# Linear attention, a top-2 mixture of experts and a feed-forward layer in one kernel: decoding spread over two steps, square sums in pieces, earlier input tiles, spread checks

## The chip, the cores and the metric

The kernel runs on one core of one Trainium2 chip. The metric is the device time of one execution in microseconds (us). TensorE (PE) multiplies matrices, VectorE (DVE) and ScalarE (ACT) work element by element, GpSimd (POOL) issues the gathering transfers and SyncE (SP) nearly all others. Each engine works through its own queue in order.

## What is computed

Three layers on 3072 tokens (4 batches of 768) of width 384: a gated linear attention with 8 heads, a mixture of 8 experts of which each token takes two, and a feed-forward layer with h - tanh(h) in place of an activation.

```python
def _attn_ref(q, k, v, f_logit):
    f = 1.0 / (1.0 + np.exp(-f_logit))
    for t in range(S):
        state = f[:, :, t, :, None] * state + np.einsum('bhd,bhe->bhde', k[:, :, t], v[:, :, t])
        y[:, :, t] = np.einsum('bhd,bhde->bhe', q[:, :, t], state)

def _moe_ref(x, w_gate, w_noise, noise, w1, w2):
    noisy_logits = x @ w_gate + np.log1p(np.exp(x @ w_noise)) * noise
    top2 = np.argpartition(-noisy_logits, 2, axis=1)[:, :2]
    ...
            h = np.maximum(x[mask] @ w1[e], 0.0)
            out[mask] += top2_w[mask, k, None] * (h @ w2[e])

def _moe2_ref(x, w_in, w_out):
    h = x @ w_in
    g = h - np.tanh(h)
    return (g @ w_out).astype(np.float32)
```

## The kernel before

The order of the work is written out by hand: each engine's queue has the instructions in the order in which the Python code issues them. Three stages follow each other.

The **attention** (lines 250 to 546) works in 24 chunks of 128 tokens and routes them on the way; the routed rows are scattered to `xs` in memory, expert by expert.

The **experts** are 128 steps (line 662): expert e, block `blk` of its 832 slots, slice f of 128 of the 1024 hidden columns. The blocks have 512 and 320 slots; in the last expert (e = 7) 320 and then 512. `moe_first` (204) makes the first product of a step, `ph`, out of nine matmuls, since every number is held as two 16-bit halves; ScalarE then writes the upper half of `hs`, VectorE the lower. `moe_second` (222) makes the second product two steps later (`LAG`), into the sums `py`; after the last slice ScalarE and VectorE move `py` to `yo`, which goes to `y_rows` in memory. Beside the products a step carries other work: `load_weights` (132) and `split_weights` (141) bring the next expert's weights into 16 buffers of two halves; `weight_sums` (148) squares them and adds up, for a check; every second step `decode_work` (582) turns 64-bit numbers of the last layer's weights into 32-bit ones: a square on ScalarE, four operations on VectorE, then for `w_in` scaling on ScalarE (591) and the lower half on VectorE, and, for the last chunk of each of three rows of tiles, a square over 2048 columns (594). For `w_out` the result goes to memory, `wo_f32`, and comes back as the weights of "expert" 8. In the last block of the last expert `gather_y` (599) fetches for each tile of 128 tokens the two experts' rows, `combine` (606) adds them with their weights, and `put_m` (612) splits the sum, has it transposed into the input tile of the feed-forward and squares it for a check.

The **second feed-forward** (line 751) has 6 blocks of 512 tokens with 16 slices each, 96 steps. In a step TensorE makes the first product of step n (`ff_first`, 621) and the second product of step n - 3 (`ff_second`, 642, `FF_LAG`). ScalarE squares `ph` to `z` and `z` to `s`, VectorE makes `s` and `g`, ScalarE the upper and VectorE the lower half of `hs` (`ff_split`, 635). The next block's four tiles are gathered at step 0 of a block, combined at 4, 6, 8 and 10 and put at 7, 9, 11 and 13. Three blocks' input tiles `xt` are held. Steps 0 to 7 also square the weights of expert 8 (764).

The fast way is only right for inputs in certain ranges; the sums are compared with bounds (`check_routes` at step 20, the rest at the end, 772 to 780), the verdicts multiplied into `ok`, added up over the partitions by a matmul, and the result is the `flag` (783). Every engine loads it and branches; where a check fails, a slow general way follows. The lines at the foot of the loop:

```python
        if n < M:
            ff_split(blk, f)
            if n < 8:
                weight_sums(NE, n)
            if n == 20:
                check_routes()
        if n < M and blk < 5 and f in (4, 6, 8, 10):
            combine(4 * blk + 4 + (f - 4) // 2)
        if n < M and blk < 5 and f in (7, 9, 11, 13):
            put_m(4 * blk + 4 + (f - 7) // 2)
```

Of the kernel before, what the change touches and what calls it, by code (L numbers as in the profile page):

```python
# [55 lines left out]
XSUM = 1.0e9  # L56
# [15 lines left out]
def fast(ctx, tc, flag, f_cols, kq_cols, v_rows, gates, blank, w12, w_in, w_out, out):  # L72
# [43 lines left out]
    isum = consts.tile([128, 3], F32, name="isum")  # L116
    xsum = consts.tile([128, 2 * NE], F32, name="xsum")
    hacc = consts.tile([128, 16 * NE], F32, name="hacc")
    msum = consts.tile([128, NT], F32, name="msum")
    junk = consts.tile([128, F2], F16, name="junk")  # L120
# [27 lines left out]
    def weight_sums(e, f):  # L148
        for i in range(2):
            nc.scalar.activation(junk[:, :DM], RING[e, f][:, 0, 3 * i:3 * i + 3, :].rearrange("p a b -> p (a b)"),  # L150
                                 AF.Square, accum_out=wsum[:, 8 * e + f, i:i + 1])
# [52 lines left out]
    def moe_first(e, blk, f):  # L204
# [376 lines left out]

    def decode_work(kind, i):
        n = 192 if kind else 256
        o = dec.tile([128, 256], F32, name="wdec")[:, :n]
        decode(o, (kind, i), n)
        if kind:
            nc.sync.dma_start(rows(wo_f32, i // 2 * 128 * DM + i % 2 * 192, [[DM, 128], [1, 192]]), o)
        else:
# [4 lines left out]
            if c == 7:  # L593
                nc.scalar.activation(junk, winS[:, 0, a, :], AF.Square, accum_out=isum[:, a:a + 1])
# [17 lines left out]
    def put_m(j):  # L612
# [6 lines left out]
        nc.scalar.activation(junk[:, :DM], g1, AF.Square, accum_out=msum[:, j:j + 1])  # L619
# [42 lines left out]
    for n in range(3, len(moe_steps) + LAG):  # L662
# [42 lines left out]
        if 4 < n < 8:  # L705
            decode_load(*loads_ahead.pop(0))
    dctx.close()
# [10 lines left out]
    def check_routes():  # L718
# [3 lines left out]
        holds(1, dv, 0.0, OP.is_lt)  # L722
        holds(4, lgs[:, :, 8:16], NMAX, OP.is_le)
# [6 lines left out]
        nc.vector.tensor_scalar(total[:, 0:1], total[:, 0:1], float(2 * N), None, op0=OP.is_equal)  # L730
# [4 lines left out]
        holds(5, sums, WSUM[0], OP.is_ge)  # L735
        holds(6, sums, WSUM[1], OP.is_le)
# [14 lines left out]
    for n in range(M + FF_LAG):  # L751
# [8 lines left out]
        if n >= FF_LAG:  # L760
            ff_second(*steps[n - FF_LAG])
# [305 lines left out]
```

## Time and profile before

| | |
|---|---|
| median of 3 runs | 996.01 us (993.24 to 997.07) |
| the profiled execution | 992.07 us, its span 990.2 us |
| granted clock of TensorE, mean | 0.985 |
| busy: PE, DVE, ACT, POOL | 948.7, 616.5, 606.6, 154.6 us |
| attention; experts; feed-forward; closing | to about 158; to 581; to 977; to 990 us |

The span is the time from the first to the last instruction of the profiled execution. A busy time is the sum over an engine's instructions; matmuls are pipelined, so two that follow each other overlap a little. The number in brackets behind a row of a timeline is the idle time ahead of it, and behind the arrow stands what ended it.

### The profile page before, as it was taken

Reading aid. Unit: us, or ns where it says so; the run is one execution under the profiler, and the core shown is the slowest. Engines: PE = TensorE matmul, PEld = TensorE weight load, DVE = VectorE, ACT = ScalarE, POOL = GpSimd, SP = SyncE. Lnnn points to the kernel's source line nnn. Section 1 sums busy time; section 2 is a strip of 40 time slices with the busy share of each in tenths; the row PEclk is TensorE's granted clock in tenths of the full one; section 3 lists DMA queues with packets and bytes.
Section 4 is the critical chain, followed back from the end, with each engine's and each line's share of the span. In section 5 each row is a group of like instructions: output and inputs, shape, how many; then the busy total and the mean of one; then the engine's idle time right before and its main releaser. Section 6 shows DMA issues by size and latency. Waiting matters only on the chain.

```text
span 990.2 us, 16233 instructions
## 1 busy us (share of the span) xinstructions
PE 948.7 (96%) x5970; PEld 580.2 (59%) x5970; DVE 616.5 (62%) x1267; ACT 606.6 (61%) x1511; POOL 154.6 (16%) x194
## 2 busy tenths in 40 slices
PE   8999999999999999999998899889899999999994
PEld 8999986555556565656565454445445555555552
DVE  7899995465555556666766434567656566666553
ACT  5777763665647475757576776654656656566552
POOL 2377776000000000000000321200201101000000
PEclk8999999999999999999999999999989999999998
DMA  7877755764636464754544341210211202100001
GB/s 256 279 239 255 257 164 169 201 188 118 193 117 194 125 180 156 178 174 143 157 140 131 77 115 53 72 56 1 73 56 37 60 33 56 41 17 17 32 1 36
DMA packets 111801, 120.04 MB, mean 121 GB/s; under 512 B 66400, under 2 KB 89568, under 8 KB 111584
## 3 DMA queue, kind: packets, MB, share of 16 engines
q1 hardware_dynamic: 105568, 100.03, 34.2%
q0 software_dynamic: 6144, 18.88, 6.0%
q8 instruction: 49, 0.80, 0.3%
q14 instruction: 40, 0.33, 0.1%
HBM read 76.41 MB, written 29.88 MB: 107 GB/s over the span
## 4 chain that ended last, share of the span: by engine, by line
PE 77%; ACT 10%; DVE 9%; DMA 2%; issue 2%; POOL 0%; SPq 0%; DVEq 0%; ACTq 0%
PE py L201 32%; PE ph L186 31%; PE pY L366 4%; PE pA L339 2%; PE pt L410 2%; PE pY L364 2%; PE pK L383 2%; ACT s L629 2%; DVE s L630 2%; DVE g L632 2%; ACT junk L150 2%; ACT hs L638 2%; ACT z L628 1%; PE pkr L352 1%; ACT hs L211 1%
## 5 line engine op out<-in xcount | busy, mean ns | idle before, releaser
L201 PE MATMUL py<-wsplit,hs 128*128 128x384 f16 x2432 | 435.2, 327 | 11.3 <-ACT yo L236 3.9
L201 PEld LDWEIGHTS <-hs 128*128 128x128 f16 x2432 | 236.9, 98 | 189.3 <-ACT hs L638 6.4
L186 PE MATMUL ph<-xt,wsplit 128*128 128x512 f16 (+3 forms) x1152 | 223.5, 339 | 0.5 <-DMA xt<-xs 0.5
L186 PE MATMUL ph<-xt,winS 128*128 128x512 f16 x864 | 205.2, 384 | 10.3 <-DMA xt<-m 9.5
L186 PEld LDWEIGHTS <-wsplit 128*128 128x128 f16 x1152 | 112.6, 98 | 86.7 <-DMA xt<-xs 0.8
L218 DVE SCALAR_TENSOR_TENSOR hs<-ph,hs 128x256 f16<-128x256 f32 (+2 forms) x192 | 79.7, 443 | 123.8 <-ACT hs L211 123.1
L638 ACT ACTIVATE hs<-g 128x512 f16<-128x512 f32 x96 | 60.4, 629 | 145.9 <-DVE g L632 145.9
L186 PEld LDWEIGHTS <-winS 128*128 128x128 f16 x864 | 84.9, 99 | 105.3 <-issue 14.4
L602 POOL DMA_INDIRECT g<-y_rows,yslot x48 | 46.5, 969 | 610.2 <-ACT junk L150 385.3
L211 ACT ACTIVATE hs<-ph 128x512 f16<-128x512 f32 (+3 forms) x128 | 65.5, 512 | 107.9 <-PE ph L186 107.4
L630 DVE SCALAR_TENSOR_TENSOR s<-s,z 128x512 f32<-128x512 f32 x96 | 66.5, 692 | 91.0 <-ACT s L629 91.0
L639 DVE TENSOR_TENSOR hs<-g,hs 128x512 f16<-128x512 f32 x96 | 66.4, 692 | 63.3 <-ACT hs L638 63.3
L145 DVE SCALAR_TENSOR_TENSOR wsplit<-raw,wsplit 128x768 f16<-128x768 f32 x72 | 70.3, 977 | 18.0 <-ACT wsplit L144 16.7
L150 ACT ACTIVATE junk<-wsplit 128x384 f16<-128x384 f16 x144 | 74.6, 518 | 2.6
L629 ACT ACTIVATE s<-z,bias_a 128x512 f32<-128x512 f32 x96 | 69.3, 722 | 3.1
L632 DVE SCALAR_TENSOR_TENSOR g<-s,ph 128x512 f32<-128x512 f32 x96 | 65.9, 687 | 3.3
L628 ACT ACTIVATE z<-ph 128x512 f32<-128x512 f32 x96 | 56.1, 584 | 12.6 <-PE ph L186 12.3
L144 ACT ACTIVATE wsplit<-raw 128x768 f16<-128x768 f32 x72 | 60.0, 833 | 1.0 <-DMA raw<-in_w 0.9
L479 POOL DMA_INDIRECT xs<-xkeep,yslot x48 | 55.2, 1151 | 15.5 <-issue 8.7
L366 PE MATMUL pY<-v,am 128*128 128x48 f32 x384 | 54.5, 271 | 0.0
L366 PEld LDWEIGHTS pY<-v,am 128*128 128x128 f32 x384 | 50.8, 196 | 0.1
L325 POOL TENSOR_TENSOR kqT<-eneg,kq 128x512 f32<-128x512 f32 x23 | 32.6, 1420 | 17.2 <-ACT eneg L321 16.9
(137 smaller groups left out, 891.9 us busy)
## 6 DMA issues: line engine op xcount, KB each, us to landing
raw<-in_w SPq DMA_DIRECT2D x64, 384.0 KB, 3.9
kq<-in_kq_cols SPq DMA_DIRECT2D x24, 512.0 KB, 5.5
y_rows<-yo SPq DMA_DIRECT2D x47, 192.0 KB, 2.3
f<-in_f_cols SPq DMA_DIRECT2D x24, 256.0 KB, 3.9
w<-in_moe_w_out SPq DMA_DIRECT2D x32, 192.0 KB, 3.5
w<-in_moe_w_in SPq DMA_DIRECT2D x24, 256.0 KB, 3.5
v<-in_v_rows SPq DMA_DIRECT2D x24, 192.0 KB, 2.6
out<-o SPq DMA_DIRECT2D x24, 192.0 KB, 1.9
```

The source lines that it names most:

```text
L145: nc.vector.scalar_tensor_tensor(t[:, 1], raw, SW, t[:, 0], op0=OP.mult, op1=OP.subtract)
L150: nc.scalar.activation(junk[:, :DM], RING[e, f][:, 0, 3 * i:3 * i + 3, :].rearrange("p a b -> p (a b)"), AF.Square, accum_out=wsum[:, 8 * ...
L186: nc.tensor.matmul(ph[:, :n], l, x[:, r, :n], start=(o == 0), stop=(o == 8))
L201: nc.tensor.matmul(p[:max(m, 128)], l, r, start=(f == 0 and o == 0), stop=(f == last and o == len(ops) - 1))
L211: nc.scalar.activation(hs[:, :n], ph[:, :n], AF.Relu, accum_out=hacc[:, at:at + 1])
L218: nc.vector.scalar_tensor_tensor(hs[:, at:at + hi - lo], ph[:, lo:hi], 0.0, hs[:, lo:hi], op0=OP.max, op1=OP.subtract)
L366: nc.tensor.matmul(pY[:, at + 48 * s:at + 48 * s + 48], am[:, s, a, :], vt[:, 2 * a + s, :], start=not c, stop=bool(s) or not c)
L629: nc.scalar.activation(s, z, AF.Square, scale=1.0 / SZ, bias=bias_a)
L630: nc.vector.scalar_tensor_tensor(s, s, ZD, z, op0=OP.add, op1=OP.mult)
L632: nc.vector.scalar_tensor_tensor(g, s, 0.5, ph, op0=OP.mult, op1=OP.mult)
L638: nc.scalar.activation(hs[:, :512], g, AF.Copy)
L639: nc.vector.tensor_tensor(hs[:, 512:], g, hs[:, :512], op=OP.subtract)
```

## The change

The arithmetic of the result stays; what moves is when and in what pieces the side work is done.

- **Decoding over two steps.** `decode_work` ends with the decoded tile and notes it in `DEC`; `decode_put`, at the next even step, stores or scales it. The squares of `w_in` are taken over 512 columns after every second chunk instead of 2048 after the last (`isum` gets four columns for each row of tiles).
- **Square sums in pieces.** The input's squares (`xsum`) come in three pieces at f = 2, 4, 6 instead of one at 7. `weight_sums` becomes `weight_sum` for one half. The 32 halves of experts 7 and 8 move into the feed-forward, one a step: at steps 13, 14, 15 and 0 of blocks and in the last block. The square in `put_m` becomes `sum_m`, at steps 9 to 12 (those of block 0's own tiles in steps 0 and 1).
- **Weights of expert 8** are split in the second half of expert 7, not the first.
- **Input tiles sooner.** `combine` at steps 1, 3, 5, 7 and `put_m` at 2, 4, 6, 8 of a block.
- **Checks** are a generator that gives one check a step in the last block; `last_check` takes the last six columns of `hsum`.
- **Flag.** The product that makes the flag stands ahead of the last second product on TensorE.

```diff
-XSUM = 1.0e9
+XSUM = 3.0e8
...
-        if f == 7:
-            nc.scalar.activation(junk[:, :3 * n].rearrange("p (a t) -> p a t", a=3), XT[e, blk][:, :3, :n], AF.Square,
-                                 accum_out=xsum[:, 2 * e + blk:2 * e + blk + 1])
+        if f in (2, 4, 6):
+            a = f // 2 - 1
+            nc.scalar.activation(junk[:, :n], XT[e, blk][:, a, :n], AF.Square,
+                                 accum_out=xsum[:, 2 * e + blk, a:a + 1])
...
+    DEC = []
+
     def decode_work(kind, i):
         n = 192 if kind else 256
         o = dec.tile([128, 256], F32, name="wdec")[:, :n]
         decode(o, (kind, i), n)
+        DEC.append((kind, i, o))
+
+    def decode_put(kind, i, o):
         if kind:
...
-            if c == 7:
-                nc.scalar.activation(junk, winS[:, 0, a, :], AF.Square, accum_out=isum[:, a:a + 1])
+            if c % 2:
+                nc.scalar.activation(junk, winS[:, 0, a, (c - 1) * 256:(c + 1) * 256], AF.Square,
+                                     accum_out=isum[:, a, c // 2:c // 2 + 1])
...
-        if blk == 1 if e == 0 else blk == 0:
+        if blk == (e in (0, NE - 1)):
             if f < 6:
                 load_weights(e + 1, f + 2)
             split_weights(e + 1, f)
-        if blk == 1:
-            weight_sums(e, f)
-            if f >= 6 and e + 2 <= NE:
+        if f >= 6:
+            if e < NE - 2 and blk == 1:
                 load_weights(e + 2, f - 6)
+            if e == NE - 1 and blk == 0:
+                load_weights(NE, f - 6)
+        if blk == 1 and e < NE - 1:
+            weight_sum(e, f, 0)
+            weight_sum(e, f, 1)
+        if DEC and not f % 2:
+            decode_put(*DEC.pop(0))
...
+        if n == M + FF_LAG - 1:
+            p = ps.tile([1, 1], F32, name="pt", tag="b7")
+            nc.tensor.matmul(p, ok, ones[:, 0:1], start=True, stop=True)
+            nc.vector.tensor_scalar(flag, p, 128.0, None, op0=OP.is_lt)
         if n >= FF_LAG:
             ff_second(*steps[n - FF_LAG])
...
+        if n >= M:
+            continue
+        ff_split(blk, f)
+        if blk < 5:
+            if f in (1, 3, 5, 7):
+                combine(ahead + f // 2)
+            if f in (2, 4, 6, 8):
+                put_m(ahead + f // 2 - 1)
+            if f in (9, 10, 11, 12):
+                sum_m(ahead + f - 9)
+        else:
+            next(checking, None)
+        if halves and (blk == 5 or f == 0 or f > 12):
+            weight_sum(*halves.pop(0))
+        if n < 2:
+            sum_m(2 * n)
+            sum_m(2 * n + 1)
+        if n == M - 1:
+            ok = last_check()
```

How instructions move, at three places. ScalarE in the first half of the last expert, two steps before the change (`hs` is the upper half, `wsplit` a weight split, `wsq` and `winS` the decoding):

```order
L211 ACTIVATE hs,hacc<-ph 128x320
L144 ACTIVATE wsplit<-raw 128x768
L211 ACTIVATE hs,hacc<-ph 128x320
L144 ACTIVATE wsplit<-raw 128x768
L575 ACTIVATE wsq<-w_6141 128x256
L591 ACTIVATE winS<-wdec 128x256
L594 ACTIVATE junk,isum<-winS 128x2048
```

and after it:

```order
L210 ACTIVATE hs,hacc<-ph 128x320
L575 ACTIVATE wsq<-w_6178 128x256
L210 ACTIVATE hs,hacc<-ph 128x320
L213 ACTIVATE junk,xsum<-xt 128x320
L596 ACTIVATE winS<-wdec 128x256
L599 ACTIVATE junk,isum<-winS 128x512
```

The scaling `winS` is no longer right behind the square `wsq` of the same chunk, but behind the next step's `hs`, and the splits are gone from here. ScalarE in the first two steps of the feed-forward before the change:

```order
L628 ACTIVATE z,hsum<-ph 128x512
L629 ACTIVATE s<-z,bias_a 128x512
L638 ACTIVATE hs<-g 128x512
L150 ACTIVATE junk,wsum<-wsplit 128x384 x2
L628 ACTIVATE z,hsum<-ph 128x512
```

and in its first four steps after it:

```order
L637 ACTIVATE z,hsum<-ph 128x512
L638 ACTIVATE s<-z,bias_a 128x512
L647 ACTIVATE hs<-g 128x512
L149 ACTIVATE junk,wsum<-wsplit 128x384
L628 ACTIVATE junk,msum<-g_6587 128x384
L628 ACTIVATE junk,msum<-g_6591 128x384
L637 ACTIVATE z,hsum<-ph 128x512
L638 ACTIVATE s<-z,bias_a 128x512
L647 ACTIVATE hs<-g 128x512
L614 ACTIVATE g_6824<-g_6824,wt 128x384
L628 ACTIVATE junk,msum<-g_6595 128x384
L628 ACTIVATE junk,msum<-g_6599 128x384
```

Two weight squares behind each of eight steps give way to one square, a combine or a put behind nearly every step; only the first two carry more. VectorE at the very end before the change (`held` and `okay` are the checks):

```order
L639 TENSOR_TENSOR hs<-g,hs 128x512
L654 TENSOR_SCALAR o<-py_9811 128x384
L654 TENSOR_SCALAR o<-py_9819 128x384
L715 TENSOR_SCALAR held<-msum 128x24
L716 TENSOR_REDUCE okay<-held 128x1
```

and after it:

```order
L648 TENSOR_TENSOR hs<-g,hs 128x512
L732 TENSOR_SCALAR held<-hsum 128x6
L733 TENSOR_REDUCE okay<-held 128x1
L737 TENSOR_TENSOR okay<-okay 128x1
L732 TENSOR_SCALAR held<-hsum 128x6
L733 TENSOR_REDUCE okay<-held 128x1
L794 TENSOR_TENSOR ok<-okay 128x1
L816 TENSOR_SCALAR flag<-pt 1x1
L663 TENSOR_SCALAR o<-py_9807 128x384
L663 TENSOR_SCALAR o<-py_9815 128x384
```

The checks stood behind the moves of the last output tiles; now the last two and the flag stand ahead of them.

## Rows read from the trace of the kernel before

**Rows 1.** The page: the span, and TensorE's part of it.

```profile
span 990.2 us, 16233 instructions
...
PE 948.7 (96%) x5970; PEld 580.2 (59%) x5970; DVE 616.5 (62%) x1267; ACT 606.6 (61%) x1511; POOL 154.6 (16%) x194
```

**Rows 2.** Waits of TensorE (PE): in total, times, longest, in us.

```profile
PE ph L186 <- DMA xt<-m: 9.5, 2, 4.7
```

**Rows 3.** Chain that ended last, 450 to 730 us: start us, us, what.

```profile
451.55 1.22 PE ph L186 x9
452.77 1.30 PE py L201 x8
...
466.68 1.94 PE ph L186 x9
...
475.11 1.95 PE py L201 x12
...
533.29 2.00 ACT junk L594 x2
```

**Rows 4.** Timeline of PE, 480 to 660 us; idle time and its releaser in brackets.

```profile
532.97 1.39 PE L186 MATMUL ph<-xt,wsplit 128*128 128x320 f16 x9
535.76 1.61 PE L201 MATMUL py<-wsplit,hs 128*128 128x384 f16 x8 [1.40 <-ACT hs L211]
...
554.03 3.68 PE L201 MATMUL py<-wsplit,hs 128*128 128x384 f16 x12 [3.88 <-ACT yo L236]
...
581.10 7.93 PE L186 MATMUL ph<-xt,winS 128*128 128x512 f16 x36
```

**Rows 5.** Timeline of ScalarE (ACT), 488 to 600 us: decoding, then the first steps.

```profile
540.45 0.42 ACT L591 ACTIVATE winS<-wdec 128x256 f16<-128x256 f32 x1 [2.54 <-DVE wdec L580]
...
583.24 0.60 ACT L628 ACTIVATE z<-ph 128x512 f32<-128x512 f32 x1 [2.12 <-PE ph L186]
...
587.33 0.52 ACT L150 ACTIVATE junk<-wsplit 128x384 f16<-128x384 f16 x1
...
587.85 0.58 ACT L628 ACTIVATE z<-ph 128x512 f32<-128x512 f32 x1
```

**Rows 6.** Timeline of PE, 640 to 730 us: the second and third block begin.

```profile
649.34 3.79 PE L186 MATMUL ph<-xt,winS 128*128 128x512 f16 x9 [4.73 <-DMA xt<-m]
...
719.56 4.00 PE L186 MATMUL ph<-xt,winS 128*128 128x512 f16 x9 [4.73 <-DMA xt<-m]
```

**Rows 7.** Busy time by stretch, 600 to 625 us (PE, PEld, DVE, ACT, POOL, PEclk, DMA).

```profile
600.00:625.00 25.00, 21.82 (x109) 9.56 (x106) 12.15 (x18) 17.28 (x46) 2.35 (x3) 1.00 0.11 26
```

**Rows 8.** Timeline of VectorE (DVE), 488 to 600 us: the feed-forward's first step.

```profile
584.71 0.69 DVE L630 SCALAR_TENSOR_TENSOR s<-s,z 128x512 f32<-128x512 f32 x1 [3.04 <-ACT s L629]
...
586.82 0.69 DVE L639 TENSOR_TENSOR hs<-g,hs 128x512 f16<-128x512 f32 x1 [0.69 <-ACT hs L638]
```

**Rows 9.** Timeline of ACT, 632 to 650 us: the feed-forward's steps 10 to 13.

```profile
633.64 0.60 ACT L608 ACTIVATE g<-g,wt 128x384 f32<-128x384 f32 x1
634.15 0.58 ACT L628 ACTIVATE z<-ph 128x512 f32<-128x512 f32 x1
...
638.50 0.57 ACT L628 ACTIVATE z<-ph 128x512 f32<-128x512 f32 x1
...
641.94 0.58 ACT L628 ACTIVATE z<-ph 128x512 f32<-128x512 f32 x1
```

**Rows 10.** Chain that ended last, 965 us to the end.

```profile
969.32 7.81 PE py L201 x48
```

**Rows 11.** Timeline of all engines, 970 us to the end.

```profile
976.21 1.89 SPq L657 DMA_DIRECT2D out<-o  x4
...
977.16 0.56 DVE L654 TENSOR_SCALAR o<-py 128x384 f32<-128x384 f32 x1 [0.42 <-PE py L201]
977.63 0.17 DVE L715 TENSOR_SCALAR held<-msum 128x24 f32<-128x24 f32 x1
...
980.16 0.15 DVE L783 TENSOR_SCALAR flag<-pt 1x1 int32<-1x1 f32 x1 [0.26 <-PE pt L782]
```

More of the change, by code (lines that the diff above doesn't have):

```diff
@@ L146, in split_weights, with weight_sum @@
         RING[e, f] = t
[L148 to L151, printed above, removed]
+    def weight_sum(e, f, i):
+        nc.scalar.activation(junk[:, :DM], RING[e, f][:, 0, 3 * i:3 * i + 3, :].rearrange("p a b -> p (a b)"),
+                             AF.Square, accum_out=wsum[:, 8 * e + f, i:i + 1])
     keep = ctx.enter_context(tc.tile_pool(name="keep", bufs=1))
@@ L618, in put_m, with sum_m @@
         nc.sync.dma_start_transpose(XT["m", j // 4][:, :, c:c + 128], m)
-        nc.scalar.activation(junk[:, :DM], g1, AF.Square, accum_out=msum[:, j:j + 1])
+        YG[j] = g1
+    def sum_m(j):
+        nc.scalar.activation(junk[:, :DM], YG.pop(j), AF.Square, accum_out=msum[:, j:j + 1])
     def ff_first(blk, f):
@@ L706, in fast @@
             decode_load(*loads_ahead.pop(0))
+    while DEC:
+        decode_put(*DEC.pop(0))
     dctx.close()
@@ L716, in holds, with both, check, checks @@
         nc.vector.tensor_reduce(okay[:, i:i + 1], held[:, :src.free_size()], axis=AX.X, op=OP.min)
-    def check_routes():
+    def both(*ts):
+        for t in ts:
+            nc.vector.tensor_tensor(okay[:, 0:1], okay[:, 0:1], t, op=OP.mult)
+    def check(i, src, bound, op):
+        holds(i, src, bound, op)
+        both(okay[:, i:i + 1])
+    def checks():
         least = small.tile([128, NT * 4], F32, name="least", bufs=1)
@@ L721, in check_routes @@
         holds(0, least, GMIN, OP.is_ge)
-        holds(1, dv, 0.0, OP.is_lt)
-        holds(4, lgs[:, :, 8:16], NMAX, OP.is_le)
+        yield
+        check(1, dv, 0.0, OP.is_lt)
+        yield
+        check(4, lgs[:, :, 8:16], NMAX, OP.is_le)
+        yield
         count = ps.tile([128, 3, NE], F32, name="pt", tag="b7")
@@ L750, in fast @@
     M = len(steps)
+    halves = [(e, f, i) for e in (NE - 1, NE) for f in range(8) for i in range(2)]
+    checking = checks()
     for n in range(M + FF_LAG):
@@ L753, in fast @@
             blk, f = steps[n]
-            if blk < 5:
-                if f == 0:
-                    for i in range(4):
-                        gather_y(4 * blk + 4 + i)
-                    new_xt(("m", blk + 1))
+            ahead = 4 * blk + 4
+            if blk < 5 and f == 0:
+                for i in range(4):
+                    gather_y(ahead + i)
+                new_xt(("m", blk + 1))
             ff_first(blk, f)
+        if n == M + FF_LAG - 1:
+            p = ps.tile([1, 1], F32, name="pt", tag="b7")
+            nc.tensor.matmul(p, ok, ones[:, 0:1], start=True, stop=True)
+            nc.vector.tensor_scalar(flag, p, 128.0, None, op0=OP.is_lt)
@@ L760, in fast @@
         if n >= FF_LAG:
             ff_second(*steps[n - FF_LAG])
-        if n < M:
-            ff_split(blk, f)
-            if n < 8:
-                weight_sums(NE, n)
-            if n == 20:
-                check_routes()
-        if n < M and blk < 5 and f in (4, 6, 8, 10):
-            combine(4 * blk + 4 + (f - 4) // 2)
-        if n < M and blk < 5 and f in (7, 9, 11, 13):
-            put_m(4 * blk + 4 + (f - 7) // 2)
-    holds(10, msum, MSUM[0], OP.is_ge)
-    holds(11, msum, MSUM[1], OP.is_le)
@@ L782, in fast @@
-    nc.tensor.matmul(p, ok, ones[:, 0:1], start=True, stop=True)
-    nc.vector.tensor_scalar(flag, p, 128.0, None, op0=OP.is_lt)
+        if n >= M:
[12 more added lines that the diff above has]
+            weight_sum(*halves.pop(0))
```

58 lines of the change are left out of this document (36 added, 22 removed).

## The prediction

> **What bounds the kernel now.** I read the page first: TensorE is busy for 948.7 of 990.2 us [rows 1], so a change can give back at most about 41 us, and only where TensorE waits or runs slowly. The waits of TensorE come next; the largest is for an input tile of the second feed-forward, 9.5 us in two waits [rows 2]. Then I asked the chain and the timeline of TensorE where the idle time lies. Ahead of 530 us the experts' chain is first product, second product, first product without a gap [rows 3]; what the change can reach lies in three places behind that.
>
> *The end of the experts.* The chain also gives what the steps cost when nothing waits: a first product 1.22 us (320 tokens) or 1.94 (512), a second product 1.30 or 1.95 [rows 3]. From 532.97 to 581.10, where the feed-forward starts [rows 4], TensorE had two first products of 320, eight of 512, four short second products and eight long ones to do: 2 x 1.22 + 8 x 1.94 + 4 x 1.30 + 8 x 1.95 = 38.8 us. It took 48.1. So 9.4 us are lost, in waits for ScalarE (1.40 and 3.88 in the rows) and in one second product after the longest wait that took 3.68 instead of 1.95. ScalarE is late because it waits 2.54 us for a decoded tile in the middle of its queue [rows 5] and then squares 2048 columns in 2.00 us [rows 3].
>
> *The second feed-forward.* A step is 1.94 + 1.95 = 3.89 us, 96 steps are 373.4 us. It runs from 581.10 to 969.32 + 7.81 = 977.13 [rows 4, 10], 396.0 us: 22.6 are lost. Two waits of 4.73 us for the transposed tile, each with a first product at half speed behind it (3.79 and 4.00 instead of 1.94), are 13.4 of it [rows 6]. The rest is ScalarE in the first block: two square sums behind each of eight steps.
>
> *The end.* After the last product at 977.13 VectorE moves the last tile out (977.16 + 0.56 = 977.72) and then makes the last checks until the flag stands at 980.31 [rows 11]; 9.9 us of closing follow, in which the rows show nothing.
>
> **ScalarE's step, the measure for what follows.** In the feed-forward ScalarE's queue is z, s, (VectorE: s, g), the upper half of hs, then extras, then the next z, so whatever stands behind hs delays every later step. A step without extras took 641.94 - 638.50 = 3.44 us, although the step before it had a put_m with its square; that one took 638.50 - 634.15 = 4.35, so copy and square are 0.91, and a combine is 634.15 - 633.64 = 0.51 [rows 9]. Two weight sums made 587.85 - 583.24 = 4.61, so 1.17 for the pair, of which the second, with the next z behind it, is 0.52 [rows 5]. TensorE's 3.89 leaves 0.45 for extras; nearly every extra is 0.05 to 0.07 over that.
>
> **The change, part by part.**
>
> *Decoding over two steps, sums in pieces.* In the first half of the last expert ScalarE no longer stands in front of VectorE's decode: its scaling comes a step later, when the tile is ready. The 2048-wide squares become four of 512, one behind every second chunk, the 16 sums over an expert's input three each, and the eight splits of the feed-forward's second weights move from that half, where a step is 1.22 + 1.30 = 2.52, to the next, where it is 3.89. The weight sums of the last expert leave the experts altogether. I take the whole 9.4 us as gained. It cannot be more, since nothing else is lost there; the other end is nothing, if ScalarE's queue stays late. The splits cost nothing beside the 1.37 us per step that the longer step gives; their loads stand on SP's queue behind transposes that wait for VectorE, but two steps, 7.8 us, ahead of their use. That cover gone is the second rival.
>
> *Input tiles three steps sooner.* combine and put_m end at step 8 of a block instead of 13, so the last transpose is issued more than seven steps ahead of the next block's first product. The four tiles are gathered on POOL's queue, which waits only for a free buffer; that is now freed by sum_m (steps 9 to 12), still ahead of the next block. Both waits of 4.73 us and the half-speed products go.
>
> *What takes their place: ScalarE.* The same extras are now spread so that almost every step has one, and 16 weight sums of the last expert are new there. From the feed-forward's start S the path of ScalarE is: first z at S + 2.14 (583.24 - 581.10); 95 steps of 3.44 = 326.8; 20 combines of 0.51 = 10.2; 20 copies and squares of 0.91 = 18.2; four more squares of 0.5 to 0.6 in steps 0 and 1, 2.3; 32 weight sums of 0.52 = 16.6. The last z stands at S + 376.2, its lower half 587.51 - 583.24 = 4.27 later [rows 5, 8], at S + 380.5. The two moves of the output tile at a block's third step fit into the time in which ScalarE waits for g. TensorE alone would begin its last second product at S + 371.4, so ScalarE sets the end by 9 us, and TensorE waits a little in every step.
>
> *Checks spread.* One check is some 0.6 us (four and the flag's product took 980.16 - 977.63 = 2.53 [rows 11]). Behind the lower half, which ends 4.27 into the step, VectorE is wanted again at 3.44 + 0.52 + 1.47 = 5.43 in a step with a weight sum (1.47 is 584.71 - 583.24, [rows 8]): single checks are hidden. In the last but one step two checks, 1.27, meet 4.91: 0.6 late. The three count products, now in the fourth step of the last block, wait for g of the step before; TensorE is at most two steps ahead of that, so they hold it 0 to 7.8 us, and as its own work has 9 us to spare by then I take nothing.
>
> *Flag ahead of the last product.* Two checks and the flag's product, half of 2.53, come between the last lower half and the last second product: 1.3. So TensorE ends at S + 380.5 + 0.6 + 1.3 + 1.95 = S + 384.3 instead of S + 396.0: 11.7 gained. Behind the last product only the move of the last tile is left ahead of the closing: 980.31 - 977.72 = 2.6 gained. If instead the closing waits for the last output transfer (1.89, [rows 11]), it is 980.31 - 979.6 = 0.7; I take 2.6, since the same transfer ended ahead of the flag before.
>
> The sum: 9.4 + 11.7 + 2.6 = 23.7 us. From the profiled execution's 992.07 that is 968.4; the median of the runs shown is 996.01, 3.9 above it, and from that it is 972.3, which I predict.
>
> On one price page and rows differ. The rows have 0.50 to 0.52 us for a square sum of 384 columns. The Trainium skill, "ScalarE: Activation LUTs", section "What ACT_TABLE_LOAD costs", gives an ACTIVATE with immediate scale and bias 186 ns + 0.833 ns per element, 93 ns of it overlapped back to back; that is an estimate of 0.41 us, and by it the 56 square sums cost some 5.6 us less and the time would be 966.7. The row holds the accumulator's read too, so I go by the row.
>
> **The rivals.**
>
> *TensorE binds throughout.* ScalarE is over the step by 0.05 to 0.07 only; if its extras partly hide, the feed-forward is 374 us, 10.3 less: 962. For it: blocks three to six had no wait. Against it: they had half as many extras, and the plain step is 3.44 wherever ScalarE was late.
>
> *The late tile moves to the feed-forward's start.* The last expert's second half now holds splits, gathers, combines and put_m together; if the first tile comes late there as it did at 649.34, it costs 4.73 + (3.79 - 1.94) = 6.6 [rows 6]: 979. Against it: before, the same tile was in time, behind a larger ScalarE queue.
>
> *The experts' end is not freed.* If the decode was not what made ScalarE late, the 9.4 stay: 982. Against it: the wait of 2.54 stands in the rows.
>
> *Slower: the clock.* In the forecast TensorE waits in nearly all of 80 steps. A half-speed product costs 3.68 - 1.95 = 1.7 to 1.9 us [rows 4, 6]; 13 of them use up the 23.7, and one in every fifth step, 16 of 1.8, gives 1001. Against it: from 600 to 625 us TensorE waited in each step, 21.82 of 25 us busy, and the granted clock was 1.00 [rows 7].
>
> **How the numbers follow.** Forecast 0.60; TensorE binds 0.17; late tile at the start 0.12; experts not freed 0.06; clock 0.05, of which 0.03 is slower than before and 0.02 within 0.5%. That bound, 5 us, is about what a measurement of this kernel can tell from no change. Faster 0.95, same 0.02, slower 0.03. The range goes from TensorE binding (962, and one below for the runs' spread) over the forecast's own 967 to 977 and the late tile to 981; left out are the last two cases and part of the first rival.
>
> **What would show it.** Right: no wait for yo or for ScalarE's hs between 530 us and the feed-forward's start, which stands near 572; no wait for xt<-m; ScalarE's z every 3.94 to 3.96 us with small waits of TensorE for hs from step 2 on; a wait for ok ahead of the last product; the flag ahead of the last tile's move. Wrong: z every 3.89 us with idle time ahead of it (TensorE binds), a wait of 2 us or more at the first step, or a granted clock under 0.95 between 600 and 900 us.

## The result and the profile after

The changed kernel takes 966.19 us in the median of 4 runs (962.48 to 970.64), the kernel before 994.62 us beside it: a ratio of 0.9717, 95% interval 0.9664 to 0.9771. Forecast were 972.3 us, between 961 and 981. The profiled execution took 962.48 us; its page begins:

```profile
span 960.7 us, 16309 instructions
...
PE 938.4 (98%) x5970; PEld 576.5 (60%) x5970; DVE 616.0 (64%) x1274; ACT 611.2 (64%) x1593; POOL 160.5 (17%) x194
```

TensorE's waits in the second feed-forward (engine, line, what it waited for: us in total, times, longest), against [rows 2]:

```profile
PE py L200 <- ACT o L665: 5.6, 1, 5.6
PE py L200 <- DVE o L663: 0.9, 3, 0.4
PE py L200 <- ACT hs L647: 0.4, 1, 0.4
PE py L200 <- DVE hs L648: 0.2, 1, 0.2
```

The waits for xt<-m, for yo and for the experts' hs are gone. A new one has come: once, for 5.6 us, a second product waits until ScalarE has moved an output tile `o` out of the sums. TensorE's timeline (start, duration, line, operation, number of products) shows where, and where the feed-forward begins:

```profile
529.83 1.39 PE L185 MATMUL ph<-xt,wsplit 128*128 128x320 f16 x9
...
534.87 2.11 PE L185 MATMUL ph<-xt,wsplit 128*128 128x512 f16 x9
...
568.61 7.93 PE L185 MATMUL ph<-xt,winS 128*128 128x512 f16 x36
...
634.00 2.11 PE L185 MATMUL ph<-xt,winS 128*128 128x512 f16 x9
...
637.95 2.11 PE L185 MATMUL ph<-xt,winS 128*128 128x512 f16 x9
645.67 1.12 PE L200 MATMUL py<-wsplit,hs 128*128 128x384 f16 x3 [5.62 <-ACT o L665]
647.21 2.54 PE L200 MATMUL py<-wsplit,hs 128*128 128x384 f16 x9 [0.42 <-DVE o L663]
649.59 2.10 PE L185 MATMUL ph<-xt,winS 128*128 128x512 f16 x9
```

534.87 is the first product over 512 tokens of the last expert; from there to the feed-forward it is 33.74 us without a gap. Before, that product stood at 539.73 and the feed-forward at 581.10 [rows 4], 41.37 us. The stretch of the 9.4 us, from the last but one product over 320 tokens to the feed-forward, takes 38.78 us (529.83 to 568.61) instead of 48.13. The rows at 645 to 650 are the second block's first second product, step 19 of the feed-forward; it and what surrounds it cost 7.7 us beyond a normal step: from that step's first product to the next one (637.95 to 649.59) it is 11.64 us, in the step before (634.00 to 637.95) 3.95. ScalarE's timeline around it:

```profile
643.82 0.58 ACT L637 ACTIVATE z<-ph 128x512 f32<-128x512 f32 x1
...
645.15 0.85 ACT L665 ACTIVATE o<-py 128x384 f32<-128x384 f32 x2
...
647.67 0.58 ACT L637 ACTIVATE z<-ph 128x512 f32<-128x512 f32 x1
...
651.73 0.60 ACT L637 ACTIVATE z<-ph 128x512 f32<-128x512 f32 x1
```

The z at 647.67 is that of step 19, whose first product ended at 640.06: ScalarE is 7.6 us late. The `o` stand in its queue in its step 18, behind `s` and ahead of `hs`, so they are as late as it is. At 651.73 z follows the next first product (649.59 + 2.10) at once: the lateness has been paid. The end, in the timeline of all engines:

```profile
950.46 0.16 PE L815 MATMUL pt<-ones,ok 128*1 128x1 bf16 x1
950.56 2.12 PE L200 MATMUL py<-wsplit,hs 128*128 128x384 f16 x12
950.66 0.15 DVE L816 TENSOR_SCALAR flag<-pt 1x1 int32<-1x1 f32 x1 [0.44 <-PE pt L815]
...
952.72 0.56 DVE L663 TENSOR_SCALAR o<-py 128x384 f32<-128x384 f32 x1 [0.42 <-PE py L200]
```

Of the 29.5 us between the two profiled spans (990.2 - 960.7), the feed-forward starts 12.5 earlier, takes 11.9 less (384.07 instead of 396.02, first product to end of the last), and 5.1 less lie behind it (8.02 instead of 13.08). Of the 12.5, 9.4 are the lost time of [rows 4]; the other 3.1 are there 32 us into the program, where the code is the same, and are the run's, not the change's (last section).

### The profile page after: what moved, and what is told of

The parts are those of the page before. It is cut to its first block, busy times and chain, and to the rows that moved or that the text cites. A ratio compares the mean times of both kernels' runs of the same rounds, so it can differ in the third digit from the quotient of the medians.

```text
span 960.7 us, 16309 instructions
## 1 busy us (share of the span) xinstructions
PE 938.4 (98%) x5970; PEld 576.5 (60%) x5970; DVE 616.0 (64%) x1274; ACT 611.2 (64%) x1593; POOL 160.5 (17%) x194
## 4 chain that ended last, share of the span: by engine, by line
PE 60%; ACT 21%; DVE 14%; issue 1%; DMA 1%; POOL 0%; SPq 0%; DVEq 0%; ACTq 0%
PE py L200 24%; PE ph L185 23%; ACT s L638 6%; DVE s L639 6%; DVE g L641 6%; ACT hs L647 5%; ACT z L637 5%; PE pY L366 4%; PE pA L339 2%; PE pt L410 2%; PE pY L364 2%; PE pK L383 2%; ACT junk L628 1%; ACT junk L149 1%; ACT g L614 1%
## 5 line engine op out<-in xcount | busy, mean ns | idle before, releaser
L185 PE MATMUL ph<-xt,winS 128*128 128x512 f16 x864 | 201.7, 379 | 0.0
L608 POOL DMA_INDIRECT g<-y_rows,yslot x48 | 52.7, 1097 | 585.1 <-ACT wsplit L144 376.0
```

Source lines behind the costliest of these rows:

```text
L185: nc.tensor.matmul(ph[:, :n], l, x[:, r, :n], start=(o == 0), stop=(o == 8))
```

## The experiments

Twelve kernels ran. Each ratio is to the kernel before as timed beside that kernel, with medians of 993.32 to 994.73 us. Times of one kernel spread over several us, and a good part of that is made in the attention, so the verdicts below rest on stretches of the profiled executions, one for each row. **E** is from the first 512-token product of the last expert to the feed-forward, **F** the feed-forward, **T** from its last product to the end of the span, all in us.

| kernel | median (range) | ratio to before [95%] | E | F | T |
|---|---|---|---|---|---|
| before | 994.62 (991.61-997.07) | 1 | 41.37 | 396.02 | 13.08 |
| changed | 966.19 (962.48-970.64) | 0.9717 [0.9664, 0.9771] | 33.74 | 384.07 | 8.02 |
| changed, again | 968.26 (964.23-970.39) | 0.9747 [0.9721, 0.9772] | 33.74 | 384.18 | 8.23 |
| decode in one step | 966.84 (965.14-970.03) | 0.9728 [0.9687, 0.9769] | 33.74 | 385.34 | 8.00 |
| splits early | 965.94 (965.04-970.22) | 0.9715 [0.9666, 0.9764] | 33.74 | 383.98 | 8.33 |
| both of these | 972.75 (969.61-978.40) | 0.9773 [0.9712, 0.9834] | 36.35 | 385.33 | 8.06 |
| sums in experts | 966.52 (963.68-967.86) | 0.9709 [0.9670, 0.9749] | 35.45 | 381.28 | 8.15 |
| late tiles | 969.65 (967.25-974.78) | 0.9731 [0.9688, 0.9774] | 33.74 | 386.79 | 8.01 |
| checks at step 20 | 972.25 (969.76-976.08) | 0.9782 [0.9730, 0.9833] | 33.74 | 388.80 | 8.02 |
| both of these | 974.73 (972.37-976.96) | 0.9816 [0.9788, 0.9844] | 33.74 | 392.28 | 8.06 |
| flag last | 970.74 (967.80-972.84) | 0.9751 [0.9710, 0.9792] | 33.74 | 385.24 | 10.89 |
| light first steps | 962.96 (957.83-964.64) | 0.9693 [0.9657, 0.9728] | 33.74 | 378.10 | 8.08 |
| the same, again | 964.36 (961.20-964.91) | 0.9709 [0.9689, 0.9729] | 33.78 | 377.64 | 8.02 |
| lighter still | 963.93 (962.25-966.64) | 0.9712 [0.9690, 0.9735] | 33.74 | 381.84 | 8.05 |

Six of these runs have the changed kernel's feed-forward, unaltered up to its last product: F is 383.98 to 385.34. Differences of F under 1.4 us say nothing.

### The experts' end: decode in one step, splits early, both

```diff
             decode_work(*todo.pop(0))
+            decode_put(*DEC.pop(0))
```

> The changed kernel with one thing undone: the scaling (or storing) of a decoded tile stands directly behind its decode again, in the same step; the 512-column squares, the splits and the weight sums stay where the change put them. Theory A, the forecast's step (ScalarE was late at the experts' end because it waited 2.54 us for a decoded tile in the middle of its queue): waits of ScalarE for wdec come back in the last expert's first half, TensorE waits for hs there, and the feed-forward starts 3 to 9 us later than the 568.6 us of the changed kernel; time 969 to 975 us. Rival B (the splits and weight sums that left these steps, or the smaller squares, made the gain): ScalarE waits for wdec but TensorE doesn't wait; the feed-forward starts within 1 us of 568.6 and the time stays at 966 within 3.

Rival B, by the waits. The groups of ScalarE's waits between 505 and 545 us hold the wait again, and TensorE doesn't feel it (E is 33.74; the one delay ahead of it is a second product of 1.69 instead of 1.46 us). The feed-forward's start, 571.26, is 2.7 us behind the 568.6 that was to hold within 1, but 2.4 of that are there already at 490 us:

```profile
ACT winS L596 <- DVE wdec L580: 10.2, 7, 2.0
```

In the kernel before the same group had 10.6 us in 7 waits, the longest 2.5. So a wait of about that size by itself isn't what made the experts' end late. The splits alone:

```diff
-        if blk == (e in (0, NE - 1)):
+        if blk == (e == 0):
             if f < 6:
                 load_weights(e + 1, f + 2)
             split_weights(e + 1, f)
```

(with the loads at f = 6 and 7 back as before)

> The changed kernel with one thing undone: the eight splits of the feed-forward's second weights stand in the last expert's first half again. The scaling of a decoded tile stays a step behind its decode. Theory A (either the splits or the wait for the decode alone fits into TensorE's steps; without the wait a pair of steps holds some 3.7 us of ScalarE's work): no wait of TensorE above 0.5 us between 500 us and the feed-forward's start, 33.74 us from the first 512-token product to it, time 966 within 3. Rival B (the place of the splits made the gain): 36 us or more, or idle time of 2 us or more ahead of that product; time 969 or more.

Theory A: no wait. And both:

> The changed kernel with two things undone in the last expert: the eight splits of the feed-forward's second weights stand in its first half again, where a step of TensorE is 2.52 us, and the scaling of a decoded tile stands directly behind its decode. The squares stay in pieces, the weight sums in the feed-forward. Theory A (ScalarE's work in a pair of steps of that half was over TensorE's 5.04 us: two hs of 0.6, two splits of 0.83, 0.4 of square and 0.4 of scaling, and the wait of 2.54 us for the decode, 6.2 in all; leaving out either the splits or the wait brings it under): both back, TensorE waits for hs in the first half; from the first 512-token product of the last expert to the feed-forward's start it is 35 to 41 us (33.74 in the changed kernel, 41.37 before), with idle time of 1 to 6 us ahead of it too. Rival B (the squares over 2048 columns, or the last expert's weight sums in its second half, made the 9.4 us): 33.74 within 0.3 and no idle time of TensorE above 0.5 us ahead.

Theory A. Now the waits for wdec, and TensorE's for ScalarE:

```profile
ACT winS L596 <- DVE wdec L580: 8.2, 6, 2.6
...
PE py L200 <- ACT hs L210: 1.7, 2, 1.0
PE py L200 <- ACT yo L236: 1.7, 2, 1.1
```

Each edit alone costs some 0.2 us at most, the two together 5.3: 2.6 of E, and 2.7 ahead of it (waits of 0.57 + 0.48 + 0.99 and slower products; ten steps take 27.89 us, 516.17 to 544.06, and 25.22 in the changed kernel). ScalarE had to be relieved of one of the two, and the change relieved it of both. In the stretch of the 9.4 us, 537.72 to 580.41 here, it is 42.69 us instead of 38.78: 3.9 of the 9.4. What the other 5.5 hung on stays open, since the squares over 2048 columns were put back in no kernel. The trace of the kernel before points at them. Each of the three stands right behind a wait for the decode, and the `hs` or `yo` that TensorE waits for next stands behind it; the first on ScalarE:

```profile
532.84 0.42 ACT L591 ACTIVATE winS<-wdec 128x256 f16<-128x256 f32 x1 [2.53 <-DVE wdec L580]
533.29 1.91 ACT L594 ACTIVATE junk<-winS 128x2048 f16<-128x2048 f16 x1
...
535.20 0.42 ACT L211 ACTIVATE hs<-ph 128x320 f16<-128x320 f32 x1
```

The second product that waited 1.40 us for this `hs` starts at 535.76 [rows 4]. Wait, scaling and square together hold `hs` up for 4.9 us here (2.53 + 0.42 + 1.91), nearly a pair of TensorE's steps, 5.04. That is a reading of one trace, not an experiment. The last expert's weight sums were put back:

```diff
-        if blk == 1 and e < NE - 1:
+        if blk == 1:
...
-halves = [(e, f, i) for e in (NE - 1, NE) for f in range(8) for i in range(2)]
+halves = [None] * 16 + [(NE, f, i) for f in range(8) for i in range(2)]
```

> The changed kernel with the 16 weight sums of the last expert put back into its second half, two a step; in the feed-forward their places stay empty, the other 16 stand where they stood. Theory A (the feed-forward's length is set by how late ScalarE is in its first block): four square sums of 0.5 us leave steps 0, 13, 14, 15, so the 6.0 us that TensorE waits at the nineteenth second product become about 4, and the feed-forward takes about 382 instead of 384.1 us. In the experts a step of 3.9 us then holds some 3.9 us of ScalarE's work, so that TensorE waits 0 to 4 us there: time 963 to 968 us. Rival B (ScalarE's sums are hidden in the feed-forward): its length stays at 384.1. Rival C (these sums in the last half were what cost the 9.4 us at the experts' end): the feed-forward starts 5 us or more later than 568.6, time 970 or more.

Theory A. These sums cost 1.7 us in the experts, as a wait for the feed-forward's first tile, and give 2.8 back in the feed-forward. The sum, 1.1 us, is under what the runs can tell: no gain of the move is shown. They alone are not the experts' 9.4 us, so rival C is out.

```profile
576.47 3.84 PE L185 MATMUL ph<-xt,winS 128*128 128x512 f16 x17 [1.49 <-DMA xt<-m]
```

### The tiles and the checks

```diff
-            if f in (1, 3, 5, 7):
-                combine(ahead + f // 2)
-            if f in (2, 4, 6, 8):
-                put_m(ahead + f // 2 - 1)
-            if f in (9, 10, 11, 12):
-                sum_m(ahead + f - 9)
+            if f in (4, 6, 8, 10):
+                combine(ahead + f // 2 - 2)
+            if f in (7, 9, 11, 13):
+                put_m(ahead + (f - 7) // 2)
+                sum_m(ahead + (f - 7) // 2)
```

> The changed kernel with one thing undone: in the feed-forward, combine stands at steps 4, 6, 8, 10 and the copy with its square at 7, 9, 11, 13 of a block again. Theory A, the forecast's step (the tile's late issue costs a wait of 4.7 us and 1.9 us of half-speed product at two block starts): two waits for the transposed tile, feed-forward some 13 us longer, 397, time 978. Theory B (the wait for the tile and the 6.0 us wait at the nineteenth second product are the same lateness of ScalarE, some 8 us at the first block's end, paid at whichever comes first; the second wait came from the checks that stood at step 20): one wait for the tile of 4 to 6 us ahead of step 16, none at step 32, the wait at the nineteenth second product under 1.5; feed-forward 383 to 387, time 965 to 969.

Theory B at the first block's end, with a smaller wait than it gave: one wait for the tile, ahead of step 16, and what was left at step 19, 1.57 us, just over its 1.5. TensorE had stood still at steps 5 and 6 for 2.0 us, put to nothing in the profile, and ScalarE had made up 3 us by that:

```profile
640.34 2.10 PE L185 MATMUL ph<-xt,winS 128*128 128x512 f16 x9 [2.77 <-DMA xt<-m]
654.80 0.65 PE L200 MATMUL py<-wsplit,hs 128*128 128x384 f16 x3 [0.68 <-ACT o L665]
656.34 1.62 PE L200 MATMUL py<-wsplit,hs 128*128 128x384 f16 x9 [0.89 <-DVE o L663]
...
673.37 2.11 PE L185 MATMUL ph<-xt,winS 128*128 128x512 f16 x9
...
719.75 1.62 PE L200 MATMUL py<-wsplit,hs 128*128 128x384 f16 x9 [0.89 <-DVE o L663]
```

F grew by 2.7 us, but not there. The first product of step 24 (673.37) stands 95.27 us behind the feed-forward's start; in the changed kernel (665.15) it is 96.54. The late tile itself cost nothing; the 2.7 us, and the 1.3 it was ahead, are lost at the ends of the later blocks, as at 719.75. There ScalarE is later again: at step 32 its z starts 2.37 us behind the end of TensorE's first product, in the changed kernel 0.43. The extras stand closer together in a block than the change spreads them. The time, 969.65, lies just above the expected 965 to 969. The checks:

```diff
-        else:
+        if n == 20:
+            for _ in range(9):
+                next(checking, None)
+        if blk == 5 and f > 8:
             next(checking, None)
```

(the nine groups at step 20, the rest in the last block from its tenth step on)

> The changed kernel with one thing undone: the checks that don't depend on the late sums (nine groups, some 7 us of VectorE, and the count products) stand at step 20 of the feed-forward again, the others in the last seven steps; the tiles stay three steps sooner. Theory B (ScalarE's lateness is made in one place and paid at the next block's end; VectorE's checks hold ScalarE's hs and z back by some 7 us, and at 3.94 us a step ScalarE doesn't make it up): TensorE waits 0.5 to 2 us behind step 20 and 3 to 6 us more at the next block's output tiles, step 35; feed-forward 388 to 391, time 970 to 973. Theory A, the forecast's step (spreading the checks gives nothing, they are hidden): feed-forward 384 within 1, time 966 within 3.

Theory B in size (F 4.7 us longer, within its 388 to 391) and in place: a wait behind step 20, and a second one at the next block's output tiles, of 1.75 + 0.89, a little under the 3 to 6 expected.

```profile
661.33 2.12 PE L185 MATMUL ph<-xt,winS 128*128 128x512 f16 x9 [2.16 <-DVE held L732]
715.80 0.65 PE L200 MATMUL py<-wsplit,hs 128*128 128x384 f16 x3 [1.75 <-ACT o L665]
```

Both together:

> The changed kernel with two things undone: combine and copy at their late steps (4 to 13 of a block), and nine groups of checks at step 20. Theory B (each lateness of ScalarE is paid once, at the next place where TensorE needs something of it): late at the first block's end, paid by a wait for the tile at step 16; made late again by the checks at step 20, paid by a second wait for the tile at step 32, as in the kernel before; feed-forward 390 to 393 us, the sum of what each cost alone (2.7 and 4.7), time 972 to 977. Theory A (two waits of 4.7 us with a half-speed product behind each, because of the late issue alone): 397 or more.

Theory B: F is 8.2 us longer, the sum of 2.7 and 4.7 within 0.8, and the kernel before's second wait for a tile is there again, which late tiles alone did not give:

```profile
633.41 4.00 PE L185 MATMUL ph<-xt,winS 128*128 128x512 f16 x9 [3.33 <-DMA xt<-m]
...
702.32 2.10 PE L185 MATMUL ph<-xt,winS 128*128 128x512 f16 x9 [1.86 <-DMA xt<-m]
```

### The flag

```diff
-        if n == M + FF_LAG - 1:
-            p = ps.tile([1, 1], F32, name="pt", tag="b7")
...
         if n >= FF_LAG:
             ff_second(*steps[n - FF_LAG])
+        if n == M + FF_LAG - 1:
+            p = ps.tile([1, 1], F32, name="pt", tag="b7")
...
```

> The changed kernel with one thing undone: the product that makes the flag, and the comparison behind it, stand behind the last second product again; the last checks stay where they are. Theory A (what follows the flag, 9.9 us in the kernel before, begins only when the flag stands, and in the changed kernel part of it runs beside the last product): from TensorE's last second product to the end of the span 8.0 us become 10.5 to 11, time 2.5 to 3 us up, 969. Rival B (the whole gain of 5.05 us at the end is the flag's place): 13 us, time 971. Rival C (only the checks that left the end made the gain): 8 us within 0.5, time 966.

Theory A: T is 10.89, 2.9 more. The flag stands 0.7 us behind the last product's end at 960.21:

```profile
960.15 0.16 PE L817 MATMUL pt<-ones,ok 128*1 128x1 bf16 x1
960.25 0.56 DVE L663 TENSOR_SCALAR o<-py 128x384 f32<-128x384 f32 x1 [0.42 <-PE py L200]
960.73 0.14 DVE L818 TENSOR_SCALAR flag<-pt 1x1 int32<-1x1 f32 x1
```

Of the 5.1 us gained at the end, 2.9 are the flag's place and 2.2 (13.08 - 10.89) the checks that no longer stand there. From the flag to the end of the span it is 9.9 us in the kernel before [rows 11] and 9.9 in the changed one (950.81 to 960.7), where the last product and its moves run beside it; with the flag last it is 10.2 (960.87 to 971.1).

### ScalarE's first steps

```diff
+        if e == NE - 1:
+            if blk == 0:
+                weight_sum(e, f, 0)
+            elif f < 4:
+                weight_sum(e, f, 1)
+                weight_sum(e, f + 4, 1)
...
                 put_m(f - 4)
+                sum_m(f - 4)
...
-        if halves and (blk == 5 or f == 0 or f > 12):
+        if halves and n >= 76:
             weight_sum(*halves.pop(0))
-        if n < 2:
-            sum_m(2 * n)
-            sum_m(2 * n + 1)
```

(`halves` holds only the second weights' sums)

> The changed kernel with ScalarE's extras taken out of the feed-forward's first steps, nothing left out: the last expert's 16 weight sums stand one a step in its first half and two a step in the first four steps of its second half, the squares of the first four input tiles directly behind their copies in the last expert, and the 16 sums of the feed-forward's second weights in steps 76 to 91, one a step. Theory A (the 6.0 us that TensorE waits at the nineteenth second product are ScalarE's lateness, 8.4 us at step 3 and 7.6 at step 19, which is made in the first steps and carried on): first z 2.1 us after the start, steps without extras 3.44 us, so ScalarE is some 3 us late at step 19 and TensorE waits about 1.3; the small waits at step 2 (0.6) go; feed-forward 378 to 379 instead of 384.1 us, time 960 to 961 if the experts' end stays without a wait. Rival B (the wait is for the output tiles' own place, not for the lateness): 5 to 6 us of wait stay, feed-forward 384, time 966. Rival C (the sums put back make the experts' end late again): feed-forward 379, but its start 3 us or more later.

Theory A in the feed-forward, to the size: F is 378.10, E stays at 33.74, and the waits at step 19 are 1.04 + 0.89. The time, 962.96, lies 2 us above the expected 960 to 961. Two rows of TensorE, and z of steps 12 to 14 on ScalarE, which follow each other by 3.94 us with a square sum between them and by 3.44 without:

```profile
642.53 0.65 PE L200 MATMUL py<-wsplit,hs 128*128 128x384 f16 x3 [1.04 <-ACT o L665]
644.07 1.62 PE L200 MATMUL py<-wsplit,hs 128*128 128x384 f16 x9 [0.89 <-DVE o L663]
```
```profile
619.04 0.57 ACT L637 ACTIVATE z<-ph 128x512 f32<-128x512 f32 x1
622.98 0.58 ACT L637 ACTIVATE z<-ph 128x512 f32<-128x512 f32 x1
626.42 0.58 ACT L637 ACTIVATE z<-ph 128x512 f32<-128x512 f32 x1
```

The changed kernel and this one again, side by side on one chip:

> The changed kernel as it is, to be compared with the next two on the same chip: 966 us within 3, feed-forward 383 to 386 us, in its first twenty steps 5 to 7 us of waits of TensorE.

> The version with ScalarE's extras taken out of the feed-forward's first steps once more, timed in more rounds beside the changed kernel. If its shorter feed-forward (378.10 instead of 384.07 us) is what counts: 5 to 6 us less than the changed kernel, 960 to 961. If the gain is lost in the spread of the runs: within 2 us of the changed kernel.

F is 384.18 and 377.64, 6.5 us apart; the medians are 968.26 and 964.36, 3.9 apart, between the two that were expected (5 to 6, or under 2), and the intervals of their ratios to before (0.9721 to 0.9772, 0.9689 to 0.9729) just touch. In both comparisons the light version is the faster one, by 3 to 4 us: likely, but near what the runs can tell. In the changed kernel's second execution TensorE stood still earlier, 1.48 + 0.35 us at step 6, put to nothing in the profile, and step 19 then waited 2.10 instead of 5.62; its waits up to there are 4.9 us, a little under the expected 5 to 7, and F is the same within 0.1. What is paid early is not paid again.

```profile
592.43 0.38 PE L185 MATMUL ph<-xt,winS 128*128 128x512 f16 x1 [1.48 <-issue]
...
648.77 1.12 PE L200 MATMUL py<-wsplit,hs 128*128 128x384 f16 x3 [2.10 <-ACT o L665]
```

One step further, four square sums out of the first block, with two more buffers:

```diff
-name=f"g{r}", bufs=6)
+name=f"g{r}", bufs=8 - 2 * r)
...
-            if f in (9, 10, 11, 12):
+            if blk and f in (9, 10, 11, 12):
                 sum_m(ahead + f - 9)
+            if blk == 1 and f > 11:
+                sum_m(f - 8)
```

> The version with light first steps, and besides the squares of the second block's four input tiles moved from steps 9 to 12 of the first block to steps 28 to 31, with two more buffers for the gathered tile. Theory A (the 1.9 us that TensorE still waits at the nineteenth second product are ScalarE's lateness too): four sums of 0.5 us go, ScalarE is some 0.8 us late at step 19, TensorE waits 0 to 0.9 there; feed-forward 376.3 to 377.5 us, time 1 to 2 us less than the version with light first steps. Rival B (what is left of the wait is the time that moving the output tiles takes): 1.5 to 2 us of wait stay, feed-forward 378.

Not decided. There is no wait at step 19, but F is 381.84: TensorE stood still several times at step 6, waiting for nothing that the profile shows, and ran at half clock there. ScalarE stood too, for 3.88 us ahead of a z, with a releaser that the profile doesn't name (remote), and that is about what F has over the 378.10 of light first steps (windows: stretch, its length, then busy time of PE, PEld, DVE, ACT, POOL, the granted clock, the share of the DMA engines, GB/s):

```profile
593.54 1.13 PE L200 MATMUL py<-wsplit,hs 128*128 128x384 f16 x3 [1.06 <-issue]
595.66 1.12 PE L200 MATMUL py<-wsplit,hs 128*128 128x384 f16 x3 [0.99 <-issue]
```
```profile
595.70 0.60 ACT L637 ACTIVATE z<-ph 128x512 f32<-128x512 f32 x1 [3.88 <-remote]
```
```profile
586.00:588.00 2.00, 2.00 (x14) 1.18 (x12) 1.27 (x3) 1.17 (x3) 1.70 (x2) 1.00 1.81 149
...
594.00:596.00 2.00, 1.01 (x5) 0.27 (x3) 0.00 (x0) 0.30 (x1) 1.64 (x2) 0.50 1.30 132
```

TensorE lost more by this stall than ScalarE, whose z stood 9.5 us behind its product at step 6 and 2.4 at step 7, so the missing wait at step 19 can't be put down to the edit.

## Why the prediction was right, and where its steps were not

The time came 6.1 us under the forecast, inside the range. Point by point:

- **Experts' end, 9.4 us: right in size, half right in cause.** TensorE has no gap there. But the forecast named the wait of 2.54 us for the decoded tile [rows 5] as the reason, and with 10.2 of its 10.6 us back nothing was lost. The wait and the early splits only hurt together, and the two make 3.9 of the 9.4 us. The forecast named the squares over 2048 columns beside the wait; they were not tried. Its list of what leaves that half was complete, so its sum held.
- **The feed-forward, 11.7 us, S + 384.3: 384.07 measured.** ScalarE's path was right to a tenth: the last z was forecast at S + 376.2 and stands at 944.72, S + 376.1. Behind step 0 ScalarE waits for a first product only at steps 20, 21 and the last, under 0.4 us in all, so the path is its own work nearly throughout. How TensorE pays for it was wrong. "TensorE waits a little in every step" came for five steps only: from step 15 to 19 the first products follow each other by 3.94 us, as z does, instead of 3.89. "Small waits for hs from step 2 on" came once, 0.36 + 0.23 at the second product of step 2. Between 587 and 640 us the timeline shows no wait; TensorE runs some 7.6 us, nearly two steps, ahead of ScalarE. It pays at a block's end, where the next sums need the place that `o` frees, and from step 20 on its steps take 3.89 again. The failed step is the sentence that the output moves "fit into the time in which ScalarE waits for g": they fit, but behind a late z they are late too, and 7.7 us are paid there at once.
- **Input tiles: gone, as forecast, but worth less.** The forecast counted 13.4 us for the two waits and their half-speed products. Putting the tiles back cost 2.7, and not at the wait that came back, but at the later blocks' ends. The first wait was ScalarE's lateness, which is otherwise paid at step 19; the second needed the checks at step 20.
- **Checks spread: costed at nothing, worth 4.7.** The forecast priced single checks in the last block, rightly as hidden, and did not ask what the checks at one step had cost before: there z of step 22 follows z of step 21 by 11.12 us (672.70 to 683.82). As the forecast took the whole feed-forward by ScalarE's new path, the sum did not suffer. Tiles and checks together are 8.2 of F's 11.95 us. The other 3.7 were put back in no kernel; by the traces it lies in the first eight steps with their pairs of weight sums, where z of step 8 stands 40.8 us behind the feed-forward's start before (621.91) and 35.9 after (604.50).
- **The flag.** The 1.3 us of checks and flag in front of the last product came (lower half to 949.28, last product at 950.56), but TensorE was still at its last second products and felt 0.3 of them as a wait for ok. Behind it 2.6 were forecast, 5.1 came: the checks' 2.2 were foreseen, the 2.9 of the flag's place were not, since the forecast let the 9.9 us of closing begin only with the last tile.
- **The square sum's price.** The rows' 0.50 to 0.52 held: z comes after 3.94 us with one and 3.44 without, and after 3.85 with a copy of the same 384 columns (643.82 to 647.67). By the Trainium skill, "ScalarE: Activation LUTs", section "What ACT_TABLE_LOAD costs", the estimate was 0.41; the copy agrees with it (3.85 - 3.44), the square sum does not, and there the measurement decides.
- **The rivals.** TensorE does not bind throughout: taking square sums away from ScalarE's first block shortened F by 6. From step 20 on it nearly does, at 3.89 us a step with ScalarE 0.05 a step over it. The late tile at the start came only when the weight sums went back (1.49). The clock's mean from 600 to 900 us was 0.99, not under the 0.95 that would have spoken against the forecast; around the one long wait, from 625 to 650 us, it was 0.86.

Between the two profiled executions 29.6 us were saved (992.07 - 962.48), 5.9 more than the forecast's 23.7: 3.1 ahead of the experts' end, which are the run's, 2.5 at the end of the kernel and 0.2 in the feed-forward; the rest is rounding. The medians' 6.1 us can't be divided like that. Of them 1.4 are the kernel before itself, whose median stood at 994.62 beside the changed one and not at the forecast's 996.01, and 2.5 the end; the rest is under the spread.

## What to carry to other kernels

When an engine runs late behind a deep queue, follow the lateness to the place where it is paid: waits at several places may be the same few microseconds, so removing one of them gains only what isn't then asked for at the next, and the cure is to lighten the steps in which the lateness is made. Two edits that each relieve the same engine can be worth nothing alone and several microseconds together, so undo both before calling either useless. What closes a kernel can begin as soon as the last branch's condition is known: make it known ahead of the last long instruction.

## What the runs showed of the hardware

In the executions profiled, the granted clock fell to its lower level (0.50) at different places ahead of 200 us, from run to run. The same windows in the kernel before and in the changed one, where the code is the same:

```profile
15.00:20.00 5.00, 5.00 (x26) 4.94 (x25) 3.97 (x6) 2.92 (x7) 1.82 (x1) 0.50 0.12 49
20.00:25.00 5.00, 5.00 (x46) 4.61 (x45) 3.32 (x6) 3.27 (x9) 2.11 (x2) 0.86 0.83 260
```
```profile
15.00:20.00 5.00, 5.00 (x52) 4.71 (x52) 5.00 (x8) 4.78 (x11) 1.88 (x2) 1.00 0.52 172
20.00:25.00 5.00, 5.00 (x52) 4.71 (x52) 4.96 (x8) 4.18 (x11) 2.24 (x3) 1.00 0.83 244
```

26 products instead of 52: half the clock for 5 us, and 46 instead of 52 in the next 5. TensorE had been busy 3.6 of the 5 us before in either. The two make the 3.1 us above. Three variants' profiles (both of the experts' edits, sums in experts, light first steps again) fell at the same place, with 25 to 27 products from 15 to 20 us; it doesn't belong to the kernel before. The first 512-token product of the last expert stood between 534.87 and 544.36 us over the profiles of the changed kernel and its variants, a spread larger than most of the effects studied here. The clock made part of it. Another part is a wait in the attention's routing, 3.4 us in the kernel with the flag last, where the code is the same as in the changed kernel, which waited 0.2 there.

TensorE's halts at steps 5 to 7 of the feed-forward, put to nothing in the profile, came in every profile but that of the kernel before and the first of the changed kernel, 0.4 to 3.6 us in all, while gathers and transposes loaded the DMA engines (a share of 1.81 and 1.30 in the windows above). In the changed kernel's first profile there was no halt from 586 to 592 us at shares of 1.18, 0.84 and 0.79 in windows of 2 us; in its second, from 589 to 595 us, it was 1.26, 0.75 and 0.77, with a halt of 1.48 us. So a load of that size alone doesn't make them; whether it has a part in them was not tried.
